# Row-form query and wo matmuls and a row-masked diagonal in a decode attention and gated-MLP kernel

## The chip, the cores and the metric

The kernel runs on one core of one Trainium2 chip. The metric is the device time of one execution in microseconds (us); lower is better. The kernel before takes 667.51 us (median of six runs, 667.38 to 667.61). All timed runs in this document have the state fast in the record (granted clock 0.749 to 0.786 of full speed), unless it is said that only one run was taken, where a state can't be told. An execution has its own span, which is 1.7 to 1.9 us shorter than the time of that run.

PE is the matmul engine, PEld its weight loads, DVE the vector engine, ACT the scalar engine, POOL the general engine, SP the engine that issues the large transfers.

## The reference

One decode step for four batch rows: attention of one query row over a cache of 4096 keys with 32 heads of 128, then a gated MLP, each with a modulation by `c`.

```python
x = A_x                                             # 4 x 1 x 512
mod = (_silu(c) @ w_mod).reshape(4, 6, 1, -1)       # sa, ca, ga, sb, cb, gb
h = _layernorm(x) * (1 + ca) + sa
q = (h @ wq).reshape(B, 1, 32, 128)...              # per head
scores = einsum('bhqd,bhkd->bhqk', q, k_cache) * 128 ** -0.5
o = einsum('bhqk,bhkd->bhqd', softmax(scores), v_cache)
x = x + ga * (o.reshape(B, 1, 4096) @ wo)
h = _layernorm(x) * (1 + cb) + sb
x = x + gb * mlp(h)                                 # gelu, layernorm, gate, w_in, w_out
```

The two caches in bf16 are 4 x 32 x 4096 x 128 x 2 bytes x 2 = 268 MB of the 282.7 MB that the kernel reads. No matrix is reused, so the kernel is one long read.

## The kernel before

The work is cut into 32 *quads*, each four heads of one batch row (8 head groups times 4 rows). A quad reads 4 MB of K and 4 MB of V, each into one of two slots. 128 partitions hold 4 heads x 32 slices of 128 keys.

```python
def scores(i, half):                       # one half of a quad
    nc.vector.tensor_tensor(out=kt, in0=kt,                          # DVE: product K * q, 4.42 us
        in1=q[:, None, :].to_broadcast([P, HT, DH]), op=ALU.mult)
    for cc in range(DH // DC):                                       # PE: 16 matmuls by the identity (32 a quad)
        nc.tensor.matmul(ps, lhsT=ident, rhs=kt[:, :, cc*DC:(cc+1)*DC], ...)

def fold(i, half):                         # DVE reduces the last eight columns: scores S
    nc.vector.tensor_reduce(out=st["S", i][:, ...], in_=st.pop(("s", i, half)), ...)

def values(i):                             # PE: 32 matmuls; big is 128 x 4 x 128
    ...
    osb = wk.tile([P, 4, DH], F32, name="osb", bufs=2)
    nc.scalar.copy(out=osb, in_=po)        # ACT

def diagonal(i):                           # PE: four fp32 matmuls pick the wanted blocks
    for n in range(4):
        nc.tensor.matmul(st["o", i], lhsT=osb[:, n, :], rhs=sel[:, NH*n:NH*n+NH],
                         start=(n == 0), stop=(n == 3))

def project(i):                            # DVE: o / sum(exp) into a column of oT
    nc.vector.reciprocal(out=rz, in_=st.pop(("z", i)))
    nc.vector.tensor_tensor(out=oT[:, :, b], in0=st.pop(("o", i)), in1=rz, op=ALU.mult)

def apply(i):                              # after the fourth row of a group
    ...
    for hl in range(NH):
        for jo in range(J):                # 16 matmuls of four columns
            nc.tensor.matmul(attn_ps[:, jo, :], lhsT=wo_g[:, hl, jo*P:(jo+1)*P],
                             rhs=oT[:, hl, :], ...)
```

The loop that sets the order on every engine.

```python
for i in range(NQ):                        # NQ = 32
    if i + 1 < NQ: st["k", i + 1] = load_k(i + 1)
    ...
    st["v", i] = load_v(i)
    if i == NQ - 1: ...                    # loads of the last wo, win, wout
    if i > 1: diagonal(i - 2)
    if i == NQ - 1: keep_busy(4)
    scores(i, 0)
    if i > 1: project(i - 2)
    scores(i, 1)
    if i == NQ - 1: softmax(i - 1)
    fold(i, 0); fold(i, 1)
    if i != NQ - 2: softmax(i)
    if i > 0: values(i - 1)
    if i > 1: apply(i - 2)
diagonal(NQ - 2); project(NQ - 2)
values_last(NQ - 1); project(NQ - 1)
# then: x1, layernorm, win, gelu, layernorm, wout, out
```

Note for later that `values(i - 1)` comes after all of quad i's scores, and `diagonal(i - 1)` comes ahead of quad i + 1's scores.

## Time and profile before

| | before |
|---|---|
| time, median of 6 runs | 667.51 us |
| span of the profiled execution | 665.9 us |
| last landing of wout, the last load | 661.25 us, 4.7 us before the end |
| last reduce of quad 31's scores ends | 642.47 us, 23.5 us before the end |
| PE, DVE, ACT busy | 410.8, 402.9, 41.3 us |
| PE instructions | 3023 matmuls, 3024 weight loads |

From the page of the kernel before: busy time of each engine, the row of the 40 equal slices for the DMA engines (busy tenths), queue lines (packets, MB, share of the 16 engines), the chain by engine, and the group of the diagonal's passes (busy us and mean ns of one; idle before it and its releaser).

```profile
PE 410.8 (62%) x3023; PEld 203.3 (31%) x3024; DVE 402.9 (60%) x475; ACT 41.3 (6%) x115; POOL 4.7 (1%) x21
DMA  9999999999999999999999999999999999999995
...
q8 instruction: 23, 0.38, 0.2%
q14 instruction: 6, 0.05, 0.0%
...
DMA 62%; PE 24%; DVE 12%; ACT 1%; issue 0%; SPq 0%; DVEq 0%
...
L354 PE MATMUL zo_ps<-sel,osb 128*128 128x4 f32 x248 | 33.1, 257 | 26.6 <-ACT osb L347 26.6
```

The DMA engines are busy in every slice but the last; no other engine is busy for two thirds of the time. So the loads bound the kernel. They run at 432 GB/s from 60 to 620 us in this trace.

The end of the chain of waits in the kernel before. Its columns are start in us, length in us, and what it was:

```profile
589.59 24.62 DMA kt<-in_A_k_cache_dram
614.23 4.43 DVE kt L276
...
618.71 8.95 PE s_ps L281 x32
...
627.78 1.87 PE big L341 x32
...
631.94 22.76 DMA wo_g<-in_A_wo_dram
...
654.74 0.60 PE attn_ps L400 x16
```

From 632 to 654.7 us the chain is one load: wo of the last group, queued behind V of quad 31. What follows it is the short computing up to the end.

### The profile page before, as it was taken

The page shows a single profiled execution, that of the slowest core. Times are in us where ns is not written, and L with a number is a line of the kernel's source. Part 1 is how long each engine was busy: PE and PEld are TensorE (multiplying, and loading weights), DVE is VectorE, ACT ScalarE, POOL GpSimd, SP SyncE. Part 2 cuts the span into 40 slices and gives each one's busy share as a digit, 9 for nine tenths or more (in the row PEclk, how much of TensorE's full clock was granted, in tenths as well). Part 3 has the DMA queues.
Part 4 walks back from the last instruction along what each step waited for, and adds up shares of the span by engine and source line. Part 5 has one row for each costly group of instructions (what it writes and reads, how often), then busy time and mean ns, then how long its engine had stood idle before and what let it go on. Part 6 is the DMA issues. An engine that isn't in the chain of part 4 may idle for free.

```text
span 665.9 us, 6937 instructions
## 1 busy us (share of the span) xinstructions
PE 410.8 (62%) x3023; PEld 203.3 (31%) x3024; DVE 402.9 (60%) x475; ACT 41.3 (6%) x115; POOL 4.7 (1%) x21
## 2 busy tenths in 40 slices
PE   2557776645676555577665577655566655557774
PEld 2223332222333222233222333222233322223344
DVE  2177766665556665556576556767555757655762
ACT  1200000000000000000000000000000000000002
POOL 2000000000000000000000000000000000000000
PEclk9988876767888667887677887766788766788885
DMA  9999999999999999999999999999999999999995
GB/s 378 433 425 432 438 434 429 427 440 432 429 428 439 432 430 428 437 428 436 429 435 428 436 431 434 426 436 433 434 431 431 434 434 426 437 432 435 426 417 228
DMA packets 12733, 283.17 MB, mean 425 GB/s; under 512 B 1432, under 2 KB 1952, under 8 KB 4000
## 3 DMA queue, kind: packets, MB, share of 16 engines
q1 hardware_dynamic: 12624, 282.73, 98.8%
q8 instruction: 23, 0.38, 0.2%
q14 instruction: 6, 0.05, 0.0%
q0 software_dynamic: 64, 0.00, 0.0%
q10 hardware_dynamic: 16, 0.01, 0.0%
HBM read 282.73 MB, written 0.00 MB: 425 GB/s over the span
## 4 chain that ended last, share of the span: by engine, by line
DMA 62%; PE 24%; DVE 12%; ACT 1%; issue 0%; SPq 0%; DVEq 0%
DMA kt<-in_A_k_cache_dram 58%; PE s_ps L281 23%; DVE kt L276 11%; DMA wo_g<-in_A_wo_dram 3%; SPq L92 0%; PE big L341 0%; PE z_ps L492 0%; DVE S L290 0%; ACT L508 0%; ACT E L311 0%; DVE P_1_109 L314 0%; DVE P_0_105 L314 0%; PE small L155 0%; PE attn_ps L400 0%; DVE mT L300 0%
## 5 line engine op out<-in xcount | busy, mean ns | idle before, releaser
L281 PE MATMUL s_ps<-kt,ident 128*128 128x512 bf16 x1024 | 289.8, 454 | 190.0 <-DVE kt L276 190.0
L276 DVE TENSOR_TENSOR kt<-kt,qbc 128x8192 bf16<-128x8192 bf16 x64 | 282.7, 4420 | 87.3 <-DMA kt<-in_A_k_cache_dram 73.4
L281 PEld LDWEIGHTS <-ident 128*128 128x128 bf16 x1024 | 115.5, 113 | 352.8 <-issue 224.2
L290 DVE TENSOR_REDUCE S<-s_ps 128x64 f32<-128x512 f32 x64 | 44.3, 692 | 120.6 <-PE s_ps L281 120.6
L354 PE MATMUL zo_ps<-sel,osb 128*128 128x4 f32 x248 | 33.1, 257 | 26.6 <-ACT osb L347 26.6
L311 ACT ACTIVATE E<-S,nm 128x128 f32<-128x128 f32 x32 | 12.8, 401 | 564.2 <-DVE nm L308 564.2
L354 PEld LDWEIGHTS zo_ps<-sel,osb 128*128 128x128 f32 x248 | 30.5, 194 | 38.4 <-ACT osb L347 38.4
L341 PE MATMUL big<-vt,P_0_105 128*32 128x512 bf16 x352 | 21.0, 380 | 1.5 <-DMA vt<-in_A_v_cache_dram 1.5
L341 PE MATMUL big<-vt,P_1_109 128*32 128x512 bf16 x320 | 19.1, 381 | 0.0
L341 PE MATMUL big<-vt,P_2_113 128*32 128x512 bf16 x320 | 19.1, 380 | 0.0
L347 ACT COPY osb<-big 128x512 f32<-128x512 f32 x31 | 17.5, 566 | 20.0 <-PE big L341 20.0
L215 PE MATMUL big<-vt,hbc 128*32 128x512 bf16 x128 | 8.9, 445 | 4.9 <-DMA vt<-in_A_wq_dram 4.9
L314 DVE TENSOR_TENSOR P_1_109<-E,mask_99 128x512 bf16<-128x512 f32 x11 | 7.6, 693 | 6.8 <-ACT E L311 6.8
L314 DVE TENSOR_TENSOR P_0_105<-E,mask_99 128x512 bf16<-128x512 f32 x11 | 7.6, 693 | 6.7 <-ACT E L311 6.7
L341 PEld LDWEIGHTS <-P_0_105 128*32 128x32 bf16 x352 | 8.4, 96 | 8.9 <-DMA vt<-in_A_v_cache_dram 1.6
L314 DVE TENSOR_TENSOR P_2_113<-E,mask_99 128x512 bf16<-128x512 f32 x10 | 6.9, 693 | 6.2 <-ACT E L311 6.2
L400 PE MATMUL attn_ps<-oP,wo_g 128*128 128x4 bf16 x112 | 3.8, 165 | 10.5 <-DVE oP L397 10.5
L375 DVE TENSOR_TENSOR oT<-zo_ps,rz 128x4 bf16<-128x4 f32 x32 | 5.4, 168 | 7.4 <-PE zo_ps L363 6.3
L341 PEld LDWEIGHTS <-P_1_109 128*32 128x32 bf16 x320 | 7.6, 96 | 6.7
L341 PEld LDWEIGHTS <-P_2_113 128*32 128x32 bf16 x320 | 7.6, 96 | 6.7
L400 PEld LDWEIGHTS <-wo_g 128*128 128x128 bf16 x128 | 4.3, 97 | 11.5 <-issue 10.4
L308 DVE STREAM_TRANSPOSE nm<-hb 128x32 f32<-128x32 f32 x32 | 6.8, 211 | 1.1
(218 smaller groups left out, 130.7 us busy)
## 6 DMA issues: line engine op xcount, KB each, us to landing
kt<-in_A_k_cache_dram SPq DMA_DIRECT2D x31, 4096.0 KB, 26.0
vt<-in_A_v_cache_dram SPq DMA_DIRECT2D x31, 4096.0 KB, 33.8
vt<-in_A_wq_dram SPq DMA_DIRECT2D x1, 4096.0 KB, 20.4
wo_g<-in_A_wo_dram SPq DMA_DIRECT2D x8, 512.0 KB, 26.2
kt<-in_A_k_cache_dram SPq DMA_DIRECT2D x2, 2048.0 KB, 25.4
vt<-in_w_mod_dram SPq DMA_DIRECT2D x1, 3072.0 KB, 10.1
vt<-in_A_v_cache_dram SPq DMA_DIRECT2D x1, 2048.0 KB, 18.5
win_434<-in_B_w_in_dram SPq DMA_DIRECT2D x1, 1344.0 KB, 24.4
```

The costliest lines, as they stand in the source:

```text
L215: nc.tensor.matmul(qp[hl * R:(hl + 1) * R, 0:n], lhsT=hbc[:, j, b, :], rhs=wv[:, g0:g0 + n, hl, :], start=(j == 0), stop=(j == J - 1), til ...
L276: nc.vector.tensor_tensor(out=kt, in0=kt, in1=q[:, None, :].to_broadcast([P, HT, DH]), op=ALU.mult,)
L281: nc.tensor.matmul(ps, lhsT=ident, rhs=kt[:, :, cc * DC:(cc + 1) * DC], start=(cc == 0), stop=(cc == DH // DC - 1),)
L290: nc.vector.tensor_reduce(out=st["S", i][:, half * HT:(half + 1) * HT], in_=st.pop(("s", i, half)), axis=AX.X, op=ALU.add,)
L308: nc.vector.transpose(out=nm, in_=hb)
L311: nc.scalar.activation(out=E, in_=S, func=AF.Exp, bias=nm[:, 0:1], scale=att_scale, accum_out=rs,)
L314: nc.vector.tensor_tensor(out=P4[:, 0:NT, :], in0=E[:, :, None].to_broadcast([P, NT, NH]), in1=mask4[:, None, :].to_broadcast([P, NT, NH]) ...
L341: nc.tensor.matmul(po[32 * t:32 * t + 32], lhsT=P4[:, n0:n0 + 8, :], rhs=st["v", i][:, n0:n0 + 4, :], start=(u == 0), stop=(u == NU - 1), ...
L347: nc.scalar.copy(out=osb, in_=po)
L354: nc.tensor.matmul(st["o", i], lhsT=osb[:, n, :], rhs=sel[:, NH * n:NH * n + NH], start=(n == 0), stop=(n == 3),)
L375: nc.vector.tensor_tensor(out=oT[:, :, b], in0=st.pop(("o", i)), in1=rz, op=ALU.mult,)
L400: nc.tensor.matmul(attn_ps[:, jo, :], lhsT=wo_g[:, hl, jo * P:(jo + 1) * P], rhs=oT[:, hl, :], start=(g == 0 and hl == 0 and jo == 0), sto ...
```

## The change

It aims to take instructions off PE in three places. (1) *Query*: 128 matmuls of 512 columns, each spreading a column of h over 32 partitions, become 32 that make q as rows and 32 that spread the rows by a selection matrix. (2) *Diagonal*: the four fp32 matmuls (eight passes: 248 records for 31 quads on the page) of each quad become four ACT copies with a row mask as scale, a DVE sum of the four blocks, and one fp32 matmul (two passes: 62 records for 31 quads on the page of the kernel after). (3) *wo*: for seven of the eight groups, 16 four-column matmuls become four of 512 columns that add up a row sum, which is turned back to columns when group six is done; the last group's wo comes in two halves. Besides, some tiles ask for 128-byte alignment.

```diff
+        for g in range(G):
+            qr = psum_s.tile([R, GW], F32, name="big", bufs=2)
+            for j in range(J):
+                nc.tensor.matmul(qr, lhsT=hz[:, j], rhs=wq[:, j, g * GW:(g + 1) * GW], ...)
+            ...                                     # cast to bf16 by DVE and ACT in turn
# query(): 16 matmuls by hbc become 4 by row_b                         [cut]
@@ values
-            nc.scalar.copy(out=osb, in_=po)
+            for n in range(4):
+                nc.scalar.activation(
+                    out=osb[:, n], in_=po[:, n], func=AF.Identity, scale=row_n[:, n:n + 1],
+                )
@@ diagonal
-            for n in range(4):
-                nc.tensor.matmul(
-                    st["o", i], lhsT=osb[:, n, :], rhs=sel[:, NH * n:NH * n + NH],
-                    start=(n == 0), stop=(n == 3),
-                )
+            osum = wk.tile([P, DH], F32, name="osum", bufs=2)
+            nc.vector.tensor_reduce(
+                out=osum, in_=osb.rearrange("p n d -> p d n"), axis=AX.X, op=ALU.add,
+            )
+            nc.tensor.matmul(st["o", i], lhsT=osum, rhs=row_h, start=True, stop=True)
@@ apply
+                for r in range(NH):
+                    nc.tensor.matmul(
+                        attn_row, lhsT=oP[:, r], rhs=wo_g[:, r],
+                        start=(g == 0 and r == 0), stop=(g == G - 2 and r == NH - 1),
+                    )
+                if g == G - 2:
+                    ar = wk.tile([B, D], F32, name="ar", bufs=1)
+                    nc.scalar.copy(out=ar, in_=attn_row[0:B])
+                    at = psum_s.tile([P, J, B], F32, name="small", bufs=1)
+                    for j in range(J):
+                        nc.tensor.matmul(at[:, j], lhsT=ar[:, j * P:(j + 1) * P], rhs=ident_f, ...)
+                    t = wk.tile([P, J, B], F32, name="ga", bufs=1)
+                    nc.vector.tensor_tensor(out=t, in0=at, in1=modT[:, 2], op=ALU.mult)
+                    nc.vector.tensor_tensor(out=xT, in0=xT, in1=t, op=ALU.add)
# the K and V slots, rows, win, wout, wo: align_bytes=128              [cut]
# the last group's wo: two tiles wo_l, two loads, 16 matmuls as before [cut]
```

More of the change, by code (lines that the diff above doesn't have):

```diff
@@ L57 @@
     wk = ctx.enter_context(tc.tile_pool(name="work", bufs=1))
-    rows = persist.tile([2 * B, D], BF16, name="rows")
+    rows = persist.tile([2 * B, D], BF16, name="rows", align_bytes=128)
     nc.scalar.dma_start(out=rows[0:B], in_=c)
@@ L70, in vslot @@
     def vslot(cols):
-        return kvp.tile([P, cols], BF16, name="vt", bufs=2)
+        return kvp.tile([P, cols], BF16, name="vt", bufs=2, align_bytes=128)
     wm = vslot(J * 6 * D)
@@ L87, in load @@
     def load(cache, i, tag, parts):
-        t = kvp.tile([P, NT * DH], BF16, name=tag, bufs=2)
+        t = kvp.tile([P, NT * DH], BF16, name=tag, bufs=2, align_bytes=128)
         a = 0
@@ L115 @@
     )
+    row_n = consts.tile([P, NH], F32, name="row_n")
+    row_h = consts.tile([P, NH], F32, name="row_h")
+    sel4 = sel[:, 0:NH * NH].rearrange("p (n h) -> p n h", h=NH)
+    nc.vector.tensor_reduce(out=row_n, in_=sel4, axis=AX.X, op=ALU.add)
+    nc.vector.tensor_reduce(
+        out=row_h, in_=sel4.rearrange("p n h -> p h n"), axis=AX.X, op=ALU.add,
+    )
     mean_d = consts.tile([P, P], F32, name="mean_d")
@@ L131, in keep_busy @@
             nc.tensor.matmul(busy_ps[0], lhsT=ident, rhs=wide, start=True, stop=True)
+    ident_f = consts.tile([B, B], F32, name="ident_f")
+    nc.vector.tensor_copy(out=ident_f, in_=ident[0:B, 0:B])
+    oPs = []
+    for a in range(2):
+        t = consts.tile([P, NH, R], BF16, name=f"oP_{a}")
+        nc.gpsimd.memset(t, 0.0)
+        oPs.append(t)
     NB = 3
@@ L185 @@
     sT = persist.tile([P, J, B], BF16, name="sT")
-    hbc = persist.tile([P, J, B, R], BF16, name="hbc")
+    hz = persist.tile([P, J, R], BF16, name="hz")
+    nc.gpsimd.memset(hz, 0.0)
+    row_b = consts.tile([R, B, R], BF16, name="row_b")
+    nc.vector.tensor_copy(out=row_b, in_=ident[0:R, 0:B, None].to_broadcast([R, B, R]))
+    WJS = [(0, J - 1), (J - 1, J)]
+    win = [
+        persist.tile([P, j1 - j0, 2 * FH], BF16, name=f"win{a}", align_bytes=128) for a, (j0, j1) in enumerate(WJS)
+    ]
+    qrow = win[0].rearrange("p j n -> p (j n)")[0:R, 0:H * DH]
     psum_acc = ctx.enter_context(
@@ L189 @@
     )
-    attn_ps = psum_acc.tile([P, J, B], F32, name="attn_ps")
+    attn_row = psum_acc.tile([R, D], F32, name="attn_row")
     psum_s = ctx.enter_context(
@@ L210, in query @@
     def query(b, g0, n, qp):
-        for j in range(J):
-            wv = wq[:, j, :].rearrange("p (g h d) -> p g h d", h=NH, d=DH)
-            for hl in range(NH):
-                nc.tensor.matmul(
-                    qp[hl * R:(hl + 1) * R, 0:n], lhsT=hbc[:, j, b, :],
-                    rhs=wv[:, g0:g0 + n, hl, :],
-                    start=(j == 0), stop=(j == J - 1),
-                    tile_position=(0, hl * R),
-                )
+        qv = qrow.rearrange("p (g h d) -> p g h d", h=NH, d=DH)
+        for hl in range(NH):
+            nc.tensor.matmul(
+                qp[hl * R:(hl + 1) * R, 0:n], lhsT=row_b[:, b, :], rhs=qv[:, g0:g0 + n, hl, :],
+                start=True, stop=True, tile_position=(0, hl * R),
+            )
     with tc.tile_pool(name="pre", bufs=1) as pre:
@@ L251 @@
         nc.vector.tensor_tensor(out=hn, in0=hn, in1=modT[:, 0], op=ALU.add)
-        nc.vector.tensor_copy(out=hbc, in_=hn[:, :, :, None].to_broadcast([P, J, B, R]))
+        nc.vector.tensor_copy(out=hz[:, :, 0:B], in_=hn)
         for oc in range(2, 6):
@@ L261 @@
             )
+        for g in range(G):
+            qr = psum_s.tile([R, GW], F32, name="big", bufs=2)
+            for j in range(J):
+                nc.tensor.matmul(
+                    qr, lhsT=hz[:, j], rhs=wq[:, j, g * GW:(g + 1) * GW],
+                    start=(j == 0), stop=(j == J - 1),
+                )
+            if g % 2 == 0:
+                nc.vector.tensor_copy(out=qrow[:, g * GW:(g + 1) * GW], in_=qr)
+            else:
+                nc.scalar.copy(out=qrow[:, g * GW:(g + 1) * GW], in_=qr)
         for b in range(B):
@@ L346, in values @@
             osb = wk.tile([P, 4, DH], F32, name="osb", bufs=2)
-            nc.scalar.copy(out=osb, in_=po)
+            for n in range(4):
+                nc.scalar.activation(
+                    out=osb[:, n], in_=po[:, n], func=AF.Identity, scale=row_n[:, n:n + 1],
+                )
             st["osb", i] = osb
@@ L352, in diagonal @@
             osb = st.pop(("osb", i))
-            for n in range(4):
-                nc.tensor.matmul(
-                    st["o", i], lhsT=osb[:, n, :], rhs=sel[:, NH * n:NH * n + NH],
-                    start=(n == 0), stop=(n == 3),
-                )
+            osum = wk.tile([P, DH], F32, name="osum", bufs=2)
+            nc.vector.tensor_reduce(
+                out=osum, in_=osb.rearrange("p n d -> p d n"), axis=AX.X, op=ALU.add,
+            )
+            nc.tensor.matmul(st["o", i], lhsT=osum, rhs=row_h, start=True, stop=True)
         def values_last(i):
@@ L384, in apply @@
                 oT = st.pop(("oT", g))
-                wo_g = st.pop(("wo", g))
-                if g < G - 1:
-                    pp = psum_s.tile([P, NH, B], F32, name="small", bufs=1)
-                    for r in range(NH):
-                        for hl in range(NH):
-                            nc.tensor.matmul(
-                                pp[hl * R:(hl + 1) * R, r, :], lhsT=ident[:, r::NH],
-                                rhs=oT[:, hl, :], start=True, stop=True,
-                                tile_position=(0, hl * R),
-                            )
-                    oT = wk.tile([P, NH, B], BF16, name="oP", bufs=2)
-                    nc.vector.tensor_copy(out=oT, in_=pp)
@@ L398, in apply @@
-                for hl in range(NH):
-                    for jo in range(J):
+                if g == G - 1:
+                    attn = psum_s.tile([P, J, B], F32, name="small", bufs=1)
+                    for hl in range(NH):
+                        for jo in range(J):
+                            nc.tensor.matmul(
+                                attn[:, jo, :], lhsT=wo_l[hl // 2][:, hl % 2, jo * P:(jo + 1) * P],
+                                rhs=oT[:, hl, :], start=(hl == 0 and jo == 0),
+                                stop=(hl == NH - 1), skip_group_check=True,
+                            )
+                    st["attn"] = attn
+                    return
@@ L400, in apply @@
+                wo_g = st.pop(("wo", g))
+                pp = psum_s.tile([P, NH, B], F32, name="small", bufs=1)
+                for r in range(NH):
+                    for hl in range(NH):
                         nc.tensor.matmul(
-                            attn_ps[:, jo, :], lhsT=wo_g[:, hl, jo * P:(jo + 1) * P], rhs=oT[:, hl, :],
-                            start=(g == 0 and hl == 0 and jo == 0),
-                            stop=(g == G - 1 and hl == NH - 1),
-                            skip_group_check=True,
-                        )
+                            pp[hl * R:(hl + 1) * R, r, :], lhsT=ident[:, r::NH],
+                            rhs=oT[:, hl, :], start=True, stop=True,
+                            tile_position=(0, hl * R),
+                        )
@@ new lines, in apply @@
+                oP = oPs[g % 2]
+                nc.vector.tensor_copy(out=oP[:, :, 0:B], in_=pp)
+                for r in range(NH):
+                    nc.tensor.matmul(
+                        attn_row, lhsT=oP[:, r], rhs=wo_g[:, r],
+                        start=(g == 0 and r == 0), stop=(g == G - 2 and r == NH - 1),
+                    )
+                if g == G - 2:
[3 more added lines that the diff above has]
+                    for j in range(J):
+                        nc.tensor.matmul(
+                            at[:, j], lhsT=ar[:, j * P:(j + 1) * P], rhs=ident_f,
+                            start=True, stop=True,
+                        )
+                    t = wk.tile([P, J, B], F32, name="ga", bufs=1)
+                    nc.vector.tensor_tensor(out=t, in0=at, in1=modT[:, 2], op=ALU.mult)
+                    nc.vector.tensor_tensor(out=xT, in0=xT, in1=t, op=ALU.add)
@@ L411 @@
         win_v = B_w_in.rearrange("(j p) n -> p j n", p=P)
-        WJS = [(0, J - 1), (J - 1, J)]
-        win = [
-            persist.tile([P, j1 - j0, F], BF16, name=f"win{a}") for a, (j0, j1) in enumerate(WJS)
-        ]
         JFS = [(0, 4), (4, JF)]
@@ L421 @@
         wout = [
-            persist.tile([P, j1 - j0, D], BF16, name=f"wout{a}") for a, (j0, j1) in enumerate(JFS)
+            persist.tile([P, j1 - j0, D], BF16, name=f"wout{a}", align_bytes=128) for a, (j0, j1) in enumerate(JFS)
         ]
+        wo_l = [wk.tile([P, NH // 2, D], BF16, name=f"wo_l{a}", bufs=1, align_bytes=128) for a in range(2)]
         st["k", 0] = load_k(0)
@@ L429 @@
                 g = quads[i][0]
-                st["wo", g] = wk.tile([P, NH, D], BF16, name="wo_g", bufs=2)
                 if g < G - 1:
+                    st["wo", g] = wk.tile([P, NH, D], BF16, name="wo_g", bufs=2, align_bytes=128)
                     nc.sync.dma_start(out=st["wo", g], in_=wo_w[g])
@@ L434 @@
             if i == NQ - 1:
-                nc.sync.dma_start(out=st["wo", G - 1], in_=wo_v[G - 1])
+                for a in range(2):
+                    nc.sync.dma_start(
+                        out=wo_l[a], in_=wo_v[G - 1, :, a * NH // 2:(a + 1) * NH // 2],
+                    )
                 for a, (j0, j1) in enumerate(WJS):
@@ L466 @@
         x1 = x1b[:, 0]
-        nc.vector.tensor_tensor(out=x1, in0=attn_ps, in1=modT[:, 2], op=ALU.mult)
+        nc.vector.tensor_tensor(out=x1, in0=st["attn"], in1=modT[:, 2], op=ALU.mult)
         nc.vector.tensor_tensor(out=x1, in0=x1, in1=xT, op=ALU.add)
```

## The prediction

> **What bounds the kernel.** The DMA engines. The page's slices show the 16 DMA engines at 90% or more in 39 of 40 slices; the stretch view gives 429 to 433 GB/s in every stretch from 60 to 640 us. A 32 KB packet takes 1213 ns throughout: 27.0 GB/s per engine, 432 for 16. [...] The 282.7 MB read need 654 us at that rate; the first packets start at 2.4 us, the last weights (wout) land at 661.3, and the span is 665.9 us. PE (62%) and DVE (60%) have slack. The chain of waits names kt transfers 58%, score matmuls 23%, DVE products 11%, but goes through slot releases that come early: a K load lands a median 26 us after issue (least 22.5) and moves for 9.7 us, so about 13 us of other loads always stand queued ahead.
>
> **What the change does.**
> - Query: 128 matmuls of 512 columns (8.9 us, 21.6 to 30.5 us) become 32 + 32. Estimate from 0.216 us per 512-column pass: 32 serial ones 6.9 us, then eight spreads paced by ACT casts (585 ns each). First qbc slice near 30 us, last near 34.5; K0 lands at 31.1. Even a wait for the last slice would slip K2's issue (44.3 us) by only 3.3 us, with queued loads landing until 51. No time.
> - Diagonal: 8 fp32 passes per quad become 2; the ACT copy (566 ns) becomes four of about 0.3 us (estimate); DVE gains a reduce of about 0.69 us (as the fold's 692 ns). PE loses about 25 us, DVE gains 21, ACT 20. Off the path: under 1 us against 13 us of queue.
> - wo: 16 four-column matmuls become 4 of 512 columns for seven groups, all before the tail.
> - Tail: the last group's wo comes in halves, so half of its 16 matmuls (0.59 us) precede the last landing: -0.3 us on x1. Then win (lands 657.96) and wout (661.25) bind again; 0.1 to 0.2 us reaches the end.
>
> **The indirect gain.** The queue table shows 23 instruction packets of 16 KB and six of 8 KB. [...] In the trace each takes about 0.93 us on one DMA engine, and the spread between the first and the last engine's increment of one transfer grows from 0.7 us at 10 us to 5.0 at the end. Every load waits for its slowest engine. The change removes about 650 PE instructions (estimate), two or three fetches[...]. What reaches the slowest engine: 0 to 1 us, expected 0.4.
>
> **Prediction: 666.9 us**, range 666.0 to 667.8. Chance of over 2% faster 0.01, within 2% 0.98, slower 0.01.
>
> **What would show it.** PE busy falls to about 375 us, DVE rises to 424, ACT to 60; PE instructions 20 or 21 packets; mean GB/s unchanged at 425; last wout landing between 660.3 and 661.5; about 4.6 us from it to the end, as before. GB/s between 40 and 60 us near 430.
>
> **What would make it wrong.** A function-table reload for the new ACT function on every quad (1.28 us each, mostly hidden); packets that take other than 1213 ns; a DMA gap near 50 us if the query takes 7 us longer; fetches that gather on one DMA engine (slower by 1 us) or leave it (faster by over 1 us).

The sum behind 666.9 us: the 667.51 us of the kernel before, less 0.4 for the fetches and 0.1 to 0.2 for the tail, with nothing for the query and the diagonal. "Two or three fetches" stands as an estimate from the page: 650 of 6047 PE instructions (3023 matmuls and 3024 weight loads) against 23 packets make 650 x 23 / 6047 = 2.5. That packets go with PE instructions was the assumption here; runs e8 and e12 test it. The 0.4 us that reach the slowest engine are an estimate too.

Its other numbers in the trace of the kernel before: 1213 ns is the median of the 8,064 packets of 32 KB (their mean, used below, is 1214.5); 0.93 us is the mean of the 23 packets of 16 KB; 0.216 us is the commonest distance between the starts of two score matmuls; 1.28 us is each of the three function-table loads. The first packet of the loads starts at 1.74 us, not at 2.4. That a load waits for its slowest engine shows at the first half of quad 31's K: the first engine's increment comes at 623.95, the last at 628.69, and the product starts at 628.72. An ACT copy of a quarter, estimated at 0.3 us, took 0.36 in the kernel after.

## More of the kernel before

The computing of quad 31 isn't in the chain. The timeline shows it:

```profile
627.70 0.69 DVE L290 TENSOR_REDUCE S<-s_ps 128x64 f32<-128x512 f32 x1 [2.76 <-PE s_ps L281]
...
628.72 4.43 DVE L276 TENSOR_TENSOR kt<-kt,qbc 128x8192 bf16<-128x8192 bf16 x1 [0.33 <-DMA kt<-in_A_k_cache_dram]
629.73 0.59 ACT L347 COPY osb<-big 128x512 f32<-128x512 f32 x1 [18.93 <-PE big L341]
630.37 1.05 PE L354 MATMUL zo_ps<-sel,osb 128*128 128x4 f32 x8 [0.75 <-ACT osb L347]
...
641.77 0.69 DVE L290 TENSOR_REDUCE S<-s_ps 128x64 f32<-128x512 f32 x1 [0.66 <-PE s_ps L281]
...
653.43 0.38 PE L363 MATMUL zo_ps<-P_1_109,vt 128*128 128x4 bf16 x8 [0.24 <-DMA vt<-in_A_v_cache_dram]
```

Quad 30's last fold starts at 627.70. Quad 31's product starts at 628.72, 1 us later, as soon as the first half of its K has landed (628.69): nothing on DVE holds it up. The diagonal of quad 29 (osb copy, eight passes) runs beside that product on ACT and PE and costs nothing. Quad 31's scores are complete at 642.47, and the last value matmuls still wait for V at 653.43.

## The result, and the profile after

| | before | after |
|---|---|---|
| time, median of 6 runs each | 667.51 (667.38 to 667.61) | 668.85 (667.81 to 670.56) |
| ratio of fast runs | | 1.0022, 95% interval 1.0007 to 1.0037 |
| span of the profiled execution | 665.9 | 666.2 |
| last landing of wout | 661.25 | 661.41 |
| last reduce of quad 31's scores ends | 642.47 | 646.50 |
| PE, DVE, ACT busy | 410.8, 402.9, 41.3 | 402.5, 437.2, 61.0 |

A ratio is the mean time of one kernel's fast runs over the mean of the other's in the same rounds, so it isn't quite the ratio of the medians in the table. The median is 1.3 us longer, above the range that was predicted, and the executions scatter over 2.8 us where those of before scatter over 0.2. The profiled execution (668.06 us) was one of the three quicker ones. Both facts need a cause.

The page of the kernel after, the lines that answer to those of before:

```profile
PE 402.5 (60%) x2698; PEld 183.1 (27%) x2698; DVE 437.2 (66%) x516; ACT 61.0 (9%) x213; POOL 5.3 (1%) x24
...
q8 instruction: 21, 0.34, 0.2%
q14 instruction: 8, 0.06, 0.0%
...
DMA 50%; PE 30%; DVE 17%; ACT 2%; issue 1%; SPq 0%; ACTq 0%; DVEq 0%
...
L394 PE MATMUL zo_ps<-row_h,osum 128*128 128x4 f32 x62 | 12.8, 277 | 67.6 <-DVE osum L391 66.9
L391 DVE TENSOR_REDUCE osum<-osb 128x128 f32<-128x512 f32 x31 | 31.6, 1021 | 7.8 <-ACT osb L382 7.1
```

Two instruction packets fewer on the first queue, two more on the other. The DVE sum takes 1.02 us. The largest change is in the chain: the share of DMA falls from 62% to 50%. The chain of waits of the kernel after, the pieces from 611 us on that matter:

```profile
611.60 1.05 PE attn_row L446 x4
612.68 0.58 ACT ar L452
613.31 1.06 PE small L455 x8
...
614.78 0.93 DVE osum L391
615.70 4.34 DVE kt L310
620.09 8.54 PE s_ps L315 x32
628.75 1.87 PE big L375 x32
630.70 1.15 ACT osb L382 x4
631.88 1.02 DVE osum L391
632.90 4.34 DVE kt L310
637.28 8.50 PE s_ps L315 x32
645.80 0.70 DVE S L324
...
648.33 1.04 ACT osb L382 x4
649.40 1.03 DVE osum L391
...
651.48 3.43 PE zo_ps L400 x128
```

From 595 us on there is no load in it. Read it from the top. The finish of wo for group six (611.60 to 614.8) and behind it an osum reduce (quad 28's) stand ahead of quad 30's product, which starts at 615.62 though its K had landed at 614.33. Then quad 30's scores; then values(29), four ACT copies and an osum of quad 29, all *ahead of quad 31's product*, which starts at 632.82 instead of 628.72, though the first half of its K landed at 628.87. Then quad 31's scores, and once more a diagonal (quad 30) ahead of the last value matmuls, which now run all 128 in a row because their V lands in time (the last piece at 653.58). The tail has become a chain of computing.

Two numbers sum up each profiled execution: where the loads end (last wout landing) and where quad 31's scores end. In none of the runs of the table behind run e10 does the kernel end less than 4.55 us after the first, nor less than 19.71 us after the second: the latter is the length of the stretch in the four profiled runs with the order of the kernel after whose chains have no load in it (after, e3, e9, e11: 19.71 to 19.75). Here, as in the tables below, landings and packet times are my reading of the trace's transfer records, and starts and ends of instructions are the timeline's. "After quad 30's scores" counts from the end of their last matmul; "scores end" is the end of the last reduce.

```
kernel    quad 30's product    quad 31's product       quad 31's scores  wout     span
          after K30 landed by  after quad 30's scores  end       to end  landed
before    (waits for K30)      1.05                    642.47    23.48   661.25   665.9
after     1.29                 4.18                    646.50    19.71   661.41   666.2
```

Before, the computing had 23.48 - 19.71 = about 3.8 us to spare (an estimate). It should be a lower bound, since the 19.7 us holds a diagonal in the new form; how long that stretch is with the old form no run shows.

### The profile page after: what moved, and what is told of

It is laid out like the page before. It is cut to its first block, busy times and chain, and to the rows that moved or that the text cites. A ratio compares the mean times of both kernels' runs of the same rounds, so it can differ in the third digit from the quotient of the medians.

```text
span 666.2 us, 6453 instructions
## 1 busy us (share of the span) xinstructions
PE 402.5 (60%) x2698; PEld 183.1 (27%) x2698; DVE 437.2 (66%) x516; ACT 61.0 (9%) x213; POOL 5.3 (1%) x24
## 4 chain that ended last, share of the span: by engine, by line
DMA 50%; PE 30%; DVE 17%; ACT 2%; issue 1%; SPq 0%; ACTq 0%; DVEq 0%
DMA kt<-in_A_k_cache_dram 47%; PE s_ps L315 27%; DVE kt L310 13%; DMA vt<-in_A_wq_dram 3%; PE big L288 1%; DVE osum L391 1%; ACT osb L382 1%; DVE S L324 1%; PE zo_ps L400 1%; ACT E L345 0%; PE big L375 0%; PE z_ps L549 0%; DVE nm L342 0%; DVE mT L334 0%; DVE hm L336 0%
## 5 line engine op out<-in xcount | busy, mean ns | idle before, releaser
L315 PE MATMUL s_ps<-kt,ident 128*128 128x512 bf16 x1024 | 292.7, 456 | 160.3 <-DVE kt L310 160.3
L345 ACT ACTIVATE E<-S,nm 128x128 f32<-128x128 f32 x32 | 12.8, 401 | 546.7 <-DVE nm L342 546.7
L394 PE MATMUL zo_ps<-row_h,osum 128*128 128x4 f32 x62 | 12.8, 277 | 67.6 <-DVE osum L391 66.9
L391 DVE TENSOR_REDUCE osum<-osb 128x128 f32<-128x512 f32 x31 | 31.6, 1021 | 7.8 <-ACT osb L382 7.1
L382 ACT ACTIVATE osb<-big,row_n 128x128 f32<-128x128 f32 x124 | 34.8, 360 | 17.4 <-PE big L375 17.4
L394 PEld LDWEIGHTS zo_ps<-row_h,osum 128*128 128x128 f32 x62 | 10.1, 205 | 82.5 <-DVE osum L391 82.5
L288 PE MATMUL big<-vt,hz 128*32 128x512 bf16 x32 | 9.3, 456 | 5.2 <-DMA vt<-in_A_wq_dram 5.2
L293 DVE CAST win_139<-big 32x512 bf16<-32x512 f32 x4 | 2.7, 678 | 11.0 <-PE big L288 11.0
L446 PE MATMUL attn_row<-wo_g,oP_105 128*32 128x512 bf16 x16 | 4.2, 382 | 6.0 <-DVE oP_105 L444 6.0
```

Of the source, the lines that this page charges most:

```text
L288: nc.tensor.matmul(qr, lhsT=hz[:, j], rhs=wq[:, j, g * GW:(g + 1) * GW], start=(j == 0), stop=(j == J - 1),)
L315: nc.tensor.matmul(ps, lhsT=ident, rhs=kt[:, :, cc * DC:(cc + 1) * DC], start=(cc == 0), stop=(cc == DH // DC - 1),)
L345: nc.scalar.activation(out=E, in_=S, func=AF.Exp, bias=nm[:, 0:1], scale=att_scale, accum_out=rs,)
L382: nc.scalar.activation(out=osb[:, n], in_=po[:, n], func=AF.Identity, scale=row_n[:, n:n + 1],)
L391: nc.vector.tensor_reduce(out=osum, in_=osb.rearrange("p n d -> p d n"), axis=AX.X, op=ALU.add,)
L394: nc.tensor.matmul(st["o", i], lhsT=osum, rhs=row_h, start=True, stop=True)
```

## The experiments

The theory after the first comparison: **order**. In the last quads no queued load hides anything, and the new operations stand on DVE ahead of a product. The rivals: **loads** (the change makes the transfers themselves slower, by the place of the slots or by instruction packets that gather on some DMA engines), and **query** (the head of the kernel is later, and stays later). The runs are named e1 to e12 in the order in which they were made. Each also had runs of the kernel before on the same chip; their medians were 667.52, 667.46 and 667.46 us in the three sets.

**Run e1. The kernel after with the old diagonal.**

```diff
-            for n in range(4):
-                nc.scalar.activation(out=osb[:, n], in_=po[:, n], func=AF.Identity, scale=row_n[:, n:n + 1])
+            nc.scalar.copy(out=osb, in_=po)
# diagonal(): the four matmuls by sel again, no osum
```

> The changed kernel with only the diagonal as it was (one ACT copy, eight fp32 passes on PE, no DVE reduce). Order theory (the reduce of quad 29 stands ahead of quad 31's product in VectorE's in-order queue, so the last quad starts about 4 us late and the tail becomes bound by compute): the product of quad 31 starts near 629 to 630 us again, runs lie within 0.3 us of each other, median 667.0 to 667.6. Rival, wo theory (group six's late row-form chain delays quad 30 by 1.3 us and the tail with it): quad 30's product still about 1.3 us behind its landing, median still above 668. Rival, DMA theory (instruction fetches or packets delay the slowest DMA engine): last wout landing and time as in the changed kernel, median above 668.

Measured: 667.83 us (667.78 to 668.05), ratio 1.0005 (0.9993 to 1.0018). The end of this run's chain of waits:

```profile
628.31 1.87 PE big L375 x32
...
631.05 21.47 DMA vt<-in_A_v_cache_dram
652.54 9.15 DMA wout<-in_B_w_out_dram
```

Quad 31's product starts 0.75 us after quad 30's scores, quad 31's scores end at 642.85, and the chain ends in loads again. The scatter is gone too: 0.27 us. So the new diagonal is needed for the loss. The finish of wo for group six still stands ahead of quad 30's product here, but without the osum behind it it holds that product only 0.38 us past its K's landing (614.38), and by itself it doesn't reach the end.

**Run e2. The kernel after with the old wo.** Column form for all eight groups, one load for the last wo.

```diff
-                    nc.tensor.matmul(attn_row, lhsT=oP[:, r], rhs=wo_g[:, r], ...)     # seven groups
+                    nc.tensor.matmul(attn_ps[:, jo, :], lhsT=wo_g[:, hl, jo * P:(jo + 1) * P], rhs=oT[:, hl, :], ...)
# no ar, ga, ident_f, oPs, wo_l
```

> The changed kernel with only wo as it was (column form for all eight groups, one wo load for the last). Order theory: quad 30's product starts at its landing, but quad 31's still starts about 3 us late (near 631.9 us), runs still scattered by over 1 us, median 668.0 to 668.7. wo theory: back to 667.0 to 667.6 with little scatter. DMA theory: no change from 668.85.

Measured: 669.67 us (669.59 to 670.07), ratio 1.0035. Slower, not quicker, and tight. It is confounded. The compiled places show that taking away some small tiles moved the K slots, too, to 128 bytes past a multiple of 256, where the V slots already were; the mean time of a 32 KB packet is 1217.8 ns (1214.5 before, 1214.8 after), and wout lands at 663.12. So this run says something of the loads, and nothing yet of wo. Runs e6 and e9 take it apart.

**Run e3. The kernel after with the old query.**

```diff
-        for g in range(G):
-            qr = psum_s.tile([R, GW], F32, name="big", bufs=2)       # and its matmuls and casts
+        for j in range(J):                                            # 16 matmuls by hbc, as before
+            ...
```

> The changed kernel with only the query as it was (128 matmuls). Order theory and wo theory: the head has 6 us of loads queued, so no change in the tail: median 668.3 to 669.4, scattered. DMA theory: one more 16 KB instruction packet (22 against 21), time up by 0 to 0.5 us. If the head mattered after all: clearly under 668.

Measured: 669.82 us (669.56 to 670.78), ratio 1.0038 (1.0025 to 1.0050), above the range that was expected. The loss stays, so the query theory falls: the new query doesn't cause it. This run also has quad 31's product 4.18 us after quad 30's scores, and quad 30's product 2.63 us after K30's landing (1.29 in the kernel after).

**Run e4. The kernel after with the last order mended.** In the last pass of the loop, the diagonal and project of quad 29 come behind quad 31's scores.

```diff
-            if i > 1:
+            if 1 < i < NQ - 1:
                 diagonal(i - 2)
 ...
             scores(i, 1)
+            if i == NQ - 1:
+                diagonal(i - 2)
+                project(i - 2)
```

> The changed kernel with one edit of order in the last iteration: the diagonal and projection of quad 29 are issued after the scores of quad 31, so the product of quad 31 stands ahead of the reduce in VectorE's queue; no work is removed. Order theory: product of quad 31 starts near 629.5 us, median 667.0 to 667.9, scatter well under 1 us unless the later reduce of quad 30 still holds the last values. wo theory and DMA theory: still above 668.

Measured: 672.24 us (670.00 to 672.79), ratio 1.0065: the slowest of all, a miss of the edit. From the timeline:

```profile
631.69 8.75 DVE L310 TENSOR_TENSOR kt<-kt,qbc 128x8192 bf16<-128x8192 bf16 x2
...
645.07 0.18 DVE L411 RECIPROCAL rz<-zo_ps 128x4 f32<-128x4 f32 x1 [3.68 <-PE zo_ps L394]
...
645.36 0.27 DVE L332 TENSOR_REDUCE mx<-S 128x1 f32<-128x128 f32 x1
```

Quad 31's product does start at once (0.64 us after quad 30's scores), as the order theory said. But the diagonal's matmul now stands on PE behind all of quad 31's scores, so the reciprocal on DVE waits for it 3.68 us, and quad 30's softmax stands behind that reciprocal. The same mistake in another place: it moved the wait instead of taking it away. DVE keeps the order here for 13.6 us: the softmax has all its data at 631.8 and begins at 645.36.

**Run e5. The old diagonal for quads 28 to 30 only, and the finish of group six behind values(29).**

```diff
+            if i >= NQ - 4:
+                nc.scalar.copy(out=osb, in_=po)          # and the four matmuls by sel in diagonal()
+                ...
# ga and xT of group six: in a function of its own, called after values(i - 1) at i == NQ - 2
```

> The changed kernel, but the last four diagonals (quads 27 to 30) take the old PE form and the transposes and two VectorE operations that finish seven groups of wo are issued one step later, after the values of quad 29. Order theory: product of quad 30 starts at its landing, product of quad 31 about 0.7 us after the scores of quad 30, scatter under 0.4 us, median 667.2 to 667.9 (the rest of the distance to before is in the loads). wo theory: the same for quad 30. DMA theory (loads alone decide): median stays above 668.

The edit reaches quads 28 to 30, not 27 to 30 as the expectation says.

Measured: 667.88 us (667.71 to 667.89), ratio 1.0006. Quad 30's product starts 0.02 us after its K has landed. Quad 31's starts 3.28 us after quad 30's scores, not about 0.7: now it is the group-six finish, put behind values(29), that DVE waits for. This placement too was a poor one. Quad 31's scores end at 645.49, and the run ends 4.55 us after wout's landing, so the loads bound it: one of the two delays alone fits into the spare time.

**Run e6. Run e2 with the K and V slots at multiples of 512.**

```diff
-        return kvp.tile([P, cols], BF16, name="vt", bufs=2, align_bytes=128)
+        return kvp.tile([P, cols], BF16, name="vt", bufs=2, align_bytes=512)
# kt likewise; the rest as in run e2
```

> The variant with only wo undone came out at 669.67 us, slower than the changed kernel, and its 32 KB packets took 1217.8 ns on average against 1214.5 before; its K and V slots start 128 bytes past a multiple of 256. Here it is the same with K and V slots placed at multiples of 512. Placement theory: packets back to about 1214.6 ns, 8064 packets on 16 engines give 1.6 us back, median about 668.1. If placement is not the cause: 669.4 to 670.0 and packets unchanged.

Measured: 667.43 us (667.32 to 668.00), ratio 1.0001 (0.9989 to 1.0014). Packets take 1214.5 ns, and wout lands at 660.95. Against run e2 the slots' place is worth 2.2 us, more than the 1.6 that the packets' length accounts for. The timeline:

```profile
630.89 1.02 DVE L384 TENSOR_REDUCE osum<-osb 128x128 f32<-128x512 f32 x1 [2.52 <-ACT osb L375]
631.83 4.42 DVE L303 TENSOR_TENSOR kt<-kt,qbc 128x8192 bf16<-128x8192 bf16 x1
...
645.11 0.69 DVE L317 TENSOR_REDUCE S<-s_ps 128x64 f32<-128x512 f32 x1 [1.14 <-PE s_ps L308]
```

Quad 31's product starts 4.18 us after quad 30's scores exactly as in the kernel after, but quad 30's starts 0.02 us after its landing. The scores end at 645.80, 19.79 us before the end, and wout lands 4.64 us before the end: both limits are met almost at once (the chain of this run still ends in loads). The new diagonal alone uses up the spare time to about 0.1 us and stops there.

**Run e9. The kernel after with the slots at multiples of 512**, so the partner of run e6 with the new wo (its halves for the last group included), and nothing else different between the two.

```diff
-        return kvp.tile([P, cols], BF16, name="vt", bufs=2, align_bytes=128)
+        return kvp.tile([P, cols], BF16, name="vt", bufs=2, align_bytes=512)
# kt likewise
```

> The changed kernel with K and V slots at multiples of 512 and nothing else. Order-plus-wo theory (the late reduce takes 3.5 us, the slack of the last quad, and group six's chain takes more than is left): the end stays 19.7 us after the last score reduce, runs scatter by over 1 us, median 668.2 to 669.2. Placement theory alone: median 667.3 to 667.6 with little scatter.

Measured: 668.93 us (667.72 to 669.47), ratio 1.0020 (1.0008 to 1.0033): the loss and the scatter of the kernel after. wout lands at 660.80, earlier than in the kernel before (661.25), and the end comes 6.36 us after it. From its timeline, the two late products:

```profile
616.57 4.42 DVE L310 TENSOR_TENSOR kt<-kt,qbc 128x8192 bf16<-128x8192 bf16 x1
...
633.76 4.41 DVE L310 TENSOR_TENSOR kt<-kt,qbc 128x8192 bf16<-128x8192 bf16 x1
```

So the loads aren't the cause of the loss, and the end no longer hangs on them.

**Run e7. The kernel before with its slots moved by 128 bytes.**

```diff
+    pad = consts.tile([P, 64], BF16, name="pad")
+    nc.gpsimd.memset(pad, 0.0)
```

> The kernel before with one unused constant of 128 bytes per partition, so that all its load targets move from a multiple of 256 to 128 past one; nothing else. Placement theory: 32 KB packets lengthen to 1216 to 1219 ns, time 668.3 to 669.5. If placement does not matter: 667.5 within 0.2.

Measured: 670.54 us (670.30 to 670.67), ratio 1.0046 (1.0033 to 1.0058), above the expected range, with nothing changed but a memset and the place of the tiles. Busy time of PE, PEld, DVE, ACT and POOL (with counts), clock, DMA share and GB/s over 60 to 620 us, for this kernel:

```profile
60.00:620.00 560.00, 354.19 (x2352) 170.11 (x2350) 350.63 (x381) 28.01 (x87) 0.00 (x0) 0.76 1.00 430
```

and for the kernel before:

```profile
60.00:620.00 560.00, 348.32 (x2347) 168.97 (x2346) 353.24 (x383) 27.99 (x87) 0.00 (x0) 0.76 1.00 432
```

A 32 KB packet takes 1218.4 ns instead of 1214.5. About 8,064 such packets over 16 engines make (1218.4 - 1214.5) x 504 = 2.0 us of the 3.1 (an estimate from these means); the first engine's share of wout lands 2.65 us later. It is the place written to that moved. Run e7 and the pair e2 and e6 (1217.8 and 1214.5 ns) agree in direction; why the place costs time is not shown. Of the K and V slots of the kernel after only the V slots are 128 past a multiple of 256, and its packets take 1214.8: why both together cost and V alone hardly does is left open.

**Run e8. The kernel before with a quarter of the value matmuls.** Its output is wrong, which doesn't matter for the time. Most of V is left out (the comparison with the reference passed its tolerance all the same). It takes away instruction packets, so it measures those.

```diff
-            NU = NT // 16
+            NU = NT // 64
```

> The kernel before with a quarter of the value matmuls (8 instead of 32 per quad), a wrong result on purpose: about 1490 fewer PE instructions, 17 or 18 instruction packets instead of 23, the same loads, and less PE work everywhere. Fetch theory (each packet of instructions delays one DMA engine[...] and the last landing waits for the slowest): the spread at the last wout landing falls from 5.0 us to about 4, time 666.2 to 667.0. If fetches do not reach the slowest engine: 667.3 to 667.6. Less PE work as such cannot help, since the loads set the end.

Measured: 667.21 us (666.88 to 667.36), ratio 0.9995 (0.9981 to 1.0008). The instruction packets on the first queue fall from 23 to 18. When V of quad 31 lands, the first and the last of the 16 DMA engines are 3.72 us apart, against 4.98 before; but then comes a fetch at 653.2 us, and at wout they are 4.68 apart. The time lies between the two forecasts. So five packets fewer give nothing that can be told from zero.

**Run e12. The kernel before with 48 more tiny matmuls per quad**, for quads 6 to 30.

```diff
+            if 5 < i < NQ - 1:
+                for _ in range(48):
+                    nc.tensor.matmul(junk, lhsT=ident[:, 0:32], rhs=wide[:, 0:B], start=False, stop=False, ...)
```

> The kernel before with 48 tiny idle matmuls (32 columns of zeros) per quad in quads 6 to 30, put where PE waits for VectorE; correct result, same loads, about 2400 more PE instructions, 32 instruction packets instead of 23. Fetch theory: the spread at the last wout landing grows from 5.0 to about 6.2 us and the time by 0.6 to 2 us (668.1 to 669.5). If fetches do not matter: 667.5 within 0.2.

Measured: 668.71 us (668.51 to 668.80), ratio 1.0018 (1.0002 to 1.0033). The line of the first instruction queue on its page:

```profile
q8 instruction: 33, 0.54, 0.3%
```

Ten packets more, 1.25 us more, the spread of the engines at wout 6.07 us (4.98 before), and the end 4.72 us after wout's landing, as before. So an instruction packet, together with the matmuls that need it, cost this load-bound kernel about 0.1 us; the run doesn't part the two, and run e8 found no such gain. The prediction's indirect effect has support from this run alone. The change takes away two packets of 16 KB on one queue and adds two of 8 KB on the other, and no gain can be seen. Queue 8's packets rose and fell with the number of PE instructions: 18 in run e8, 21 in the kernel after, 23 before, 33 here.

**Run e11. The kernel after, unchanged, once more**, for a second profile of a slower execution.

> The changed kernel once more, one look, to see another of its scattered executions. Order-plus-wo theory: whatever its time between 667.8 and 670.6, the end stands 19.7 us (within 0.3) after the last score reduce of quad 31, and the landing of the last wout stays at 661.4 (within 0.3). Load theory: the last wout landing moves with the time instead.

One run, so its state is unknown: 669.12 us, span 667.4 (the first profile: 668.06 and 666.2). From its timeline, the transposes of group six's sum, quad 31's product and its last reduce:

```profile
613.83 1.76 PE L455 MATMUL small<-ident_f,ar 4*128 4x4 f32 x8 [0.66 <-ACT ar L452]
...
633.98 4.42 DVE L310 TENSOR_TENSOR kt<-kt,qbc 128x8192 bf16<-128x8192 bf16 x1
...
646.94 0.69 DVE L324 TENSOR_REDUCE S<-s_ps 128x64 f32<-128x512 f32 x1 [0.81 <-PE s_ps L315]
```

In the first profile the same transposes took 1.05 us and that reduce began at 645.80. The granted clock from 608 to 616 us was 0.87 here and 1.00 there. From the reduce's end to the end of the kernel it is 19.73 us, against 19.71; wout lands at 661.40, against 661.41. In both, quad 29's product starts when its K has landed (594.88 here, 594.91 there), so the whole difference of 1.2 us arises in computing between 595 and 647 us: 0.5 us by the end of quad 29's scores, where the granted clock was 0.74 against 0.80, and 0.7 in these transposes. So where the chain is computing, the clock that PE is granted shows in the time. This explains two executions; the rest of the scatter is argued from them.

**Run e10. Both remedies, placed better.** Old diagonal for quads 29 and 30 only (quad 31 has none), the group-six finish put off to the last pass ahead of values(30), slots at multiples of 512. The rest is the kernel after; the cut of the edit below is against run e5.

```diff
-            if i >= NQ - 4:
+            if i >= NQ - 3:
 ...
+            if i == NQ - 1:
+                seven_groups()                    # ga and xT of group six, ahead of values(i - 1)
-            if i == NQ - 2:
-                seven_groups()                    # behind values(i - 1)
# vt and kt: align_bytes=512
```

> The changed kernel with both repairs of the tail (PE-form diagonal for quads 29 and 30; the transposes that finish seven groups of wo issued in the last iteration after its softmax) and K and V slots at multiples of 512. All theories together: product of quad 31 about 0.7 to 1.1 us after the scores of quad 30, loads bind the end again, scatter under 0.3 us, median 667.1 to 667.5, so at best 0.4 us faster than before. If something else in the change costs time: above 667.7.

Measured: 667.47 us (667.29 to 667.51), ratio 0.9999 (0.9987 to 1.0012). From the timeline of this run, quad 31's product and the last reduce of its scores:

```profile
629.35 4.42 DVE L310 TENSOR_TENSOR kt<-kt,qbc 128x8192 bf16<-128x8192 bf16 x1
...
642.09 0.69 DVE L324 TENSOR_REDUCE S<-s_ps 128x64 f32<-128x512 f32 x1 [0.59 <-PE s_ps L315]
```

Quad 31's product starts 0.64 us after quad 30's scores, and wout's landing (661.08) is 4.55 us before the end. It still has the new query, the new diagonal in 29 quads and wo in row form; loss and scatter are gone. Against run e9, whose slots are at the same place, only the two remedies of the tail differ, and they are worth 1.46 us: this pair is the plainest proof that the order in the last quads is the cause. It equals the kernel before and doesn't beat it, because the loads set both.

The runs that matter, side by side. The four with both a late product of quad 30 and a late product of quad 31 are the four over 668.5 us (not in the table: run e2, whose loads are slower, and run e4, which moved the wait):

```
run                        time     quad 30's     quad 31's product   scores 31  wout     end less
                           median   product       after quad 30's     end        landed   wout
                                    starts        scores
before                     667.51   614.23        1.05                642.47     661.25   4.69
after                      668.85   615.62        4.18                646.50     661.41   4.79
e3  old query              669.82   617.16        4.18                648.09     661.40   6.43
e9  after, slots at 512    668.93   616.57        4.18                647.44     660.80   6.36
e11 after again (one run)  669.12   616.86        4.18                647.63     661.40   5.95
e1  old diagonal           667.83   614.76        0.75                642.85     661.68   4.55
e5  finish moved, old diag 667.88   614.54        3.28                645.49     661.38   4.55
e6  old wo, slots at 512   667.43   614.05        4.18                645.80     660.95   4.64
e10 both out of the tail   667.47   614.37        0.64                642.78     661.08   4.55
```

## Why the prediction was wrong

**What held.** The loads bound the kernel before and through the steady part of the kernel after (432 GB/s from 60 to 620 us in both). The last wout landing, predicted between 660.3 and 661.5, was 661.41. ACT was predicted at 60 us busy and measured 61.0. The query part cost nothing: its row matmuls took longer than estimated (9.3 us for 32 of them, against 6.9), the first product began at 31.95 instead of 31.20, K2 was issued 0.65 us later, and from 40 to 60 us the loads ran at 446 GB/s; run e3 shows that the new query isn't the loss. The two halves of wo did give the last 0.1 us: where loads bind, the end is 4.55 us after wout (runs e1 and e10) instead of 4.69.

**The step that failed, first.** "Off the path: under 1 us against 13 us of queue." That is true of 29 quads (run e10 keeps the new diagonal there and loses nothing) and false of the last ones. Behind quad 31's V and the small weights there is no queue, so the delay isn't absorbed by it; what absorbs is the spare time between computing and the last loads, about 3.8 us, which the prediction never read. And the delay isn't the cost of the reduce. Before, quad 29's diagonal ran on ACT and PE beside quad 31's product. Now its sum stands on DVE *ahead of* the product, and it has to wait for values(29) (1.91 us), four ACT copies (1.14) and itself (1.02): 4.18 us after quad 30's scores instead of 1.05, and 3.95 us after its K has landed. Run e6 shows that these 3.1 us just fit. The mis-sized term, a reduce estimated at 0.69 us that took 1.02, is the smaller part.

**The step that failed, second.** "wo: 16 four-column matmuls become 4 of 512 columns for seven groups, all before the tail." The matmuls are; the finish isn't. Group six is done at the end of pass 29, and its row sum goes PE, ACT, PE, DVE (611.60 to 614.8 in the kernel after) ahead of quad 30's product, which starts 1.3 us after its K in one profile and 2.6 us in another (run e3). Part of that is the first step again: DVE takes quad 28's osum (1.01 us) only behind the finish. In run e6, without the finish, that sum is done at 612.4, before the K lands; in run e1, without the sum, the finish holds quad 30 only 0.38 us, and this alone doesn't reach the end.

**Together.** Both are needed. With slots at the same place, new wo against old wo on top of the new diagonal costs 668.93 - 667.43 = 1.5 us (runs e9 and e6); new diagonal against old on top of the new wo costs 668.85 - 667.83 = 1.0 us (after and run e1). Without either in the tail the time is that of before (run e10 against e9, 1.46 us). Also wrong for that reason: "about 4.6 us from it to the end, as before" (4.79 in a quick execution, 5.95 and 6.36 in slower ones), and the narrow range, since the chain of computing went with PE's granted clock (1.2 us between the two profiled executions of run e11).

**The gain that didn't come.** "What reaches the slowest engine: 0 to 1 us, expected 0.4." PE's packets fell to 21 as predicted, other fetches rose by two, and the spread of the engines at wout was 5.16 us, not below 4.98. Whether the mechanism holds stays open: run e12 speaks for it (ten packets more, 1.25 us), run e8 shows nothing.

**PE and DVE busy** were off: 402.5 us against about 375, and 437.2 against 424. One part is that the eight passes cost 33.1 us before and the two cost 12.8 in their place, 20 us less instead of 25, and that the DVE sum is 31.6 us instead of 21. Most of the rest of PE's difference lies where fewer instructions took more time: wo of the seven groups 7.3 us in 28 matmuls of 512 columns, against 3.8 in 112 of four columns; the query 12.4 us (9.3 for the rows, the rest for the spreads) against 8.9; and the score matmuls, which weren't changed, 292.7 against 289.8.

**Left open.** Runs e1 and e5 are 0.3 to 0.4 us above the kernel before, with wout landing at 661.68 and 661.38. The slots' place is one candidate, as run e10 with slots at 512 hasn't got it (661.08); no run isolates it. The effect of the slots' place in runs e2 and e7 is measured, its cause isn't. The fold (512 fp32 elements a partition to 64, read from the matmuls' tile) took 692 ns, the strided sum (512 to 128, read from ACT's tile) 1021 ns; no run tells whether the strides, the place or the number of results makes the difference.

## What to carry to other kernels

In this load-bound kernel the new diagonal was free in 29 quads (run e10, 667.47 us) and cost 1.0 us through the last ones (668.85 against 667.83, run e1). So look up in the last pass how long the computing could wait before it becomes what ends last, and compare that with the delay, not with the share of busy time. When work moves to an engine that holds the chain's next step, ask what stands ahead of that step in its order and what *that* waits for; here DVE passed on the wait, not just the cost (a sum of 1.02 us made quad 31's product 3.1 us later). If the executions of a kernel begin to scatter where they didn't (2.8 us here against 0.2), suspect that something other than the loads now ends last.
